# Memory values as column strips on widened probabilities, and token values moved between two projections

## The chip, the cores and the metric

The kernel runs on one core of a Trainium2 chip. Its engines, by the profile's names, are PE (TensorE matmul) with PEld (TensorE weight load), DVE (VectorE), ACT (ScalarE), POOL (GpSimd) and SP (SyncE, which here only issues DMAs). The metric is device time in microseconds for one execution, as the median of several runs. About 0.3% is what a measurement of this kernel tells from no change.

## The reference, cut to what matters

A recurrent attention layer with memory goes over 2048 tokens in 64 segments of 32. Each segment's input is 8 memory rows followed by its 32 tokens. The 8 memory rows of the output are the next segment's memory, so the segments depend on each other. A feed-forward layer with a squared relu follows over all tokens. B = 1, Dm = D = 640, H = 32 heads, Dh = 128, M = 8, seg = 32, F = 1728, all bfloat16.

```python
idx = jnp.arange(L)                      # L = M + seg_len = 40
mask = (idx[:, None] < M) | (idx[:, None] >= idx[None, :])
mem = mem0
for s in range(n_seg):
    xs = x[:, s * seg_len:(s + 1) * seg_len, :]
    h = jnp.concatenate([mem, xs], axis=1)
    q = jnp.einsum('btd,dhe->bhte', h, Wq)
    k = jnp.einsum('btd,dhe->bhte', h, Wk)
    v = jnp.einsum('btd,dhe->bhte', h, Wv)
    scores = jnp.einsum('bhqe,bhke->bhqk', q, k) * scale
    scores = jnp.where(mask[None, None], scores, -1000000000.0)
    p = _softmax(scores, axis=-1)
    o = jnp.einsum('bhqk,bhke->bhqe', p, v)
    o = jnp.einsum('bhte,hed->btd', o, Wo)
    mem = o[:, :M, :]
    outs.append(o[:, M:, :])
...
# then: h = x + attention(layernorm(x)); out = h + relu(layernorm(h) @ w1 + b1)**2 @ w2 + b2
```

## The kernel before

**Stages.** `start()` projects the first segment and the first tails. Then comes a loop of 64 calls of `step(b, sp)`, one for each segment (s = 4b + sp), and last the feed-forward layer in four blocks of 512 tokens (line 918 on). Every engine runs its instructions in the order in which the program writes them (`manual_schedule`, line 109), so the order of the lines is the order in each engine's queue. The number of copies of a tile (`bufs`) and the data decide what waits.

**Rows of a step.** A segment's 40 rows are split into 32 (8 memory rows and the first 24 tokens, the "main" rows) and 8 (the last tokens, the "tail"). The main rows are projected in the step itself. The tails of four segments are projected together, one block ahead, by small units that stand in a list `fill` and are put between other matmuls by `run(fill, n)`. Lists `late`, `mid` and `owed` hold pieces for the other engines, to be run at later places.

**Two forms of matmul.** The 128 x 128 array is used in strips. A projection, a score or a product with Wo loads 128 x 32 weights (written `128*32` in the profile) and four of them work side by side on four column strips. The values (probabilities times v) use `32*128`: 32 rows of v, four side by side on four row strips, one for each group g of 8 heads. Heads are in G = 4 groups of HG = 8, and the partitions 32g to 32g + 31 of a softmax tile hold group g. Two halves n = 0, 1 hold 16 heads each.

**Order of a step on TensorE.** Projections q0, k0, q1, k1 (`project`, line 471: 20 matmuls of 512 columns each, copied out by ACT, turned by DVE into qT and kT). Memory scores of half 0 (`scores(0)`, line 492), v half 0 up to c = 2, token scores of half 0, the rest of v half 0, v half 1 up to c = 2, memory and token scores of half 1, v half 1 c = 2. Then `values(0)`, the rest of v half 1, one fill unit, six rounds of Wo over heads of half 0 (`wo_rounds(main, pw, 0, 6)`, line 619), the token values of the segment before (`token_values(s - 1)`, line 426), `values(1)`, the remaining Wo rounds with fill units between, and more fill units, while DVE and ACT turn the 8 new memory rows into the next step's input (`mem_to_hT`, line 291). The next q0 needs these.

**Memory probabilities.** Only the 8 memory rows' results are needed at once. `soft1(n)` (line 501) takes the maximum on DVE and the exponential on ACT into em (128 x 40: 32 main keys, 8 tail keys), with its sum read out to zm. `soft2(n)` (line 510) on DVE: reciprocal, scale of the main part, a product that spreads the 8 tail keys over 4 x 8 places under the mask `same`, and a 32 x 32 block transpose to pT (128 x 64). `values(n, pT, po)` (line 522) multiplies: for each of 4 heads j and 4 groups g, 32 rows of v times 8 columns of pT; then 4 matmuls for the tail keys with `vt4`, the tail rows' values fetched back from DRAM. `values_out` (line 536) copies po to oT, for n = 0 on DVE, for n = 1 on ACT. Token probabilities take the whole next stretch: tk, mxk on DVE (lines 611 to 615), ek on ACT, zk and rk on DVE, pkt and pk on POOL (lines 632 to 645), turned by DVE in the next step (`owed`, lines 654 to 660). They are used one step later.

**PSUM.** `mm` has three banks in turn, `chn` one for memory scores and the Wo sums `pw`, `po` (four banks) the values.

**Padding.** `align` (line 122) counts the TensorE instructions issued and lets `proj` split some 512-column matmuls into two of 256, so that the number of instructions before a fixed place in each step is a multiple of 256 plus a set number (`PLACE`).

Of the kernel before, what the change touches and what calls it, by code (L numbers as in the profile page):

```python
# [16 lines left out]
def kernel(  # L17
# [16 lines left out]
    nc = tc.nc  # L34
# [44 lines left out]
    o_ring = [const.tile([64, DH], BF16, name="o%d" % k) for k in range(5)]  # L79
# [20 lines left out]
    nc.vector.tensor_copy(out=same[:], in_=diag[:].unsqueeze(2).to_broadcast([128, 4, TL]))  # L100
    qT = const.tile([128, H, NK], BF16)
# [10 lines left out]
    BLOCK, AHEAD, PLACE = 256, 65, 34  # L112
# [189 lines left out]
    fill, late, mid, owed = [], [], [], [[], [], []]  # L302
# [123 lines left out]
    def token_values(s, v, vt4, po, opens):  # L426
# [3 lines left out]
        for i in range(HG):  # L430
            for g in range(G):
                r = slice(32 * g, 32 * g + 32)
                matmul(po[:, g, i * 32:(i + 1) * 32], lhsT=v[r, i * E:(i + 1) * E], rhs=pTk[r, i, :],
                                 start=(opens and i == 0), stop=False, skip_group_check=True)
# [24 lines left out]
    def step(b, sp, v=None):  # L459
# [5 lines left out]
        if not ready:  # L465
            v = vs.pop(0) if vs else s2.tile([128, EG], BF16, tag="v", name="v")
        run(late, 10 if b in (0, NB - 2, NB - 1) else 2)
# [33 lines left out]
        def soft1(n):  # L501
            mx = s2.tile([128, 1], F32, tag="mx", name="mx")
            nc.vector.tensor_reduce(out=mx[:], in_=sms[n][:, 0:NK], op=ALU.max, axis=AX.X, negate=True)  # L503
            em = s2.tile([128, NK], BF16, tag="em", name="em")
            zm = s2.tile([128, 1], F32, tag="zm", name="zm")
            nc.scalar.activation(out=em[:], in_=sms[n][:, 0:NK], func=ACT.Exp, bias=mx[:, 0:1], scale=1.0,  # L506
                                 accum_out=zm[:])
            ems[n], zms[n] = em, zm

        def soft2(n):  # L510
            rm = s2.tile([128, 1], F32, tag="rm", name="rm")
            nc.vector.reciprocal(out=rm[:], in_=zms[n][:])
            pm = s2.tile([128, 2 * SEG], BF16, tag="pmem", name="pmem")
            nc.vector.tensor_scalar(out=pm[:, 0:SEG], in0=ems[n][:, 0:SEG], scalar1=rm[:, 0:1], scalar2=None, op0=ALU.mult)
            nc.vector.scalar_tensor_tensor(out=pm[:, SEG:2 * SEG].rearrange("p (j k) -> p j k", k=TL),
                                           in0=ems[n][:, SEG:NK].unsqueeze(1).to_broadcast([128, 4, TL]),
                                           scalar=rm[:, 0:1], in1=same[:], op0=ALU.mult, op1=ALU.mult)
            pT = s2.tile([128, 2 * SEG], BF16, tag="pTm", name="pTm")
            nc.vector.transpose(out=pT[:], in_=pm[:])
            return pT  # L520

        def values(n, pT, po):
            c0 = 256 + n * 4 * M
            for j in range(4):
                i = n * 4 + j
                for g in range(G):
                    r = slice(32 * g, 32 * g + 32)
                    matmul(po[:, g, c0 + j * M:c0 + (j + 1) * M], lhsT=v[r, i * E:(i + 1) * E],
                                     rhs=pT[r, j * M:(j + 1) * M], start=(i == 0), stop=False,
                                     skip_group_check=True)  # L530
            for g in range(G):
                r = slice(32 * g, 32 * g + 32)
                matmul(po[:, g, c0:c0 + 4 * M], lhsT=vt4[r, sp, n, :], rhs=pT[r, 32:64],
                                 start=False, stop=True, skip_group_check=True)

        def values_out(n, po):
            c0 = 256 + n * 4 * M
            evac(n == 0, oTg[:, n, :, :, 0:M], po[:, :, c0:c0 + 4 * M].rearrange("p g (j m) -> p g j m", m=M))

        if not ready and not last:  # L540
            align(s + b, 4 * 8 * DC + 32 + 1 + 16)
# [3 lines left out]
        run(owed[0], 2)  # L545
        if not last:
            project("k", wk, kT, 0)
        run(owed[1], 2)
        run(late, 1)
        project("q", wq, qT, 1)  # L550
        if last:
# [5 lines left out]
        run(owed[2], 1)  # L557
# [40 lines left out]
        po = pop.tile([128, G, 512], F32, tag="po", name="po")  # L598
        if not ready:
            proj(wv, "half", lhs, 1, ps1, 2, 3)  # L600
        if not last:
            values(0, pT0, po)
            values_out(0, po)
# [11 lines left out]
        nc.vector.tensor_tensor(out=tk[:], in0=tk[:], in1=mxk[:].unsqueeze(2).to_broadcast([128, HG, NK]), op=ALU.subtract)  # L615

        pw = chn.tile([128, 512], F32, tag="ch", name="pw")
        main = lambda p: oT[:, p, 0:32]
        wo_rounds(main, pw, 0, 6)
        if s:  # L620
            token_values(s - 1, prev["v"], prev["vt4"], po, last)
        if not last:
            values(1, pT1, po)
            values_out(1, po)
        wo_rounds(main, pw, 6, 8)
# [7 lines left out]
        nc.scalar.activation(out=ek[:], in_=tk[:], func=ACT.Exp, scale=1.0)  # L633
        zk = s1.tile([128, HG], F32, tag="zk", name="zk")
        nc.vector.tensor_reduce(out=zk[:], in_=ek[:], op=ALU.add, axis=AX.X)  # L635
        if not last:
            mem_to_hT(pw, hT4s[(s + 1) // 4], (s + 1) % 4)
# [8 lines left out]
        if s:  # L646
            owed[0].append(lambda: token_out(0, po))
            owed[1].append(lambda: token_out(1, po))
# [13 lines left out]
        if not last:  # L662
            tails_in((s + 1) // 4, (s + 1) % 4)
# [178 lines left out]
    for b in range(NB):  # L842
        for sp in range(4):
# [34 lines left out]
            if b > 0 and sp == 1 and b + 1 < NB:  # L878
                late.append(lambda b=b: ln_norm(b + 1))
# [29 lines left out]
    token_values(NS - 1, prev["v"], prev["vt4"], po, True)  # L909
# [105 lines left out]
```

## Time and profile before

| what | value |
| --- | --- |
| median of 3 runs | 958.0 us (956.51 to 959.76) |
| the profiled execution, its own time | 958.06 us |
| its span on the core | 956.3 us |
| PE matmul time in the span | 929.1 us, 97% |
| DVE, ACT, POOL busy | 699.7, 548.4, 258.2 us |
| granted TensorE clock | 1.000 |
| a step of the loop (479.70 to 515.80 holds three) | 12.28, 11.95, 11.87 us |
| longest waits of the PE | 12.3 us at the start (xn), 4.8 us for hT over five steps, 1.4, 1.4 and 1.1 us once each |

The profile has one line for each group of instructions. The program's own matmul helper records every matmul, so all matmuls have the line L116, and they are told apart by the tiles they write and read: `ps<-wq,hT` is a projection, `sm<-kT,qz` memory scores, `ps<-kT,qT` token scores, `po<-pTm,v` memory values, `po<-pTk,v` token values (`pTx,vt` and `pTm,vt` their tail keys), `pw<-wo,oT` the product with Wo. A matmul's end is modelled, so the time that TensorE loses between two matmuls is read from where the next one starts, not from its idle time. In the timeline, neighbouring instructions of one group are merged into a line with its count; the columns are start, length, engine, line, operation, tiles and shapes, and in brackets idle time before it and what ended it.

### The profile page before, as it was taken

The numbers are of one execution on the slowest core, as the hardware profiler recorded it, in microseconds if no ns is written. First come the engines' busy times: TensorE is split into PE (matmuls) and PEld (weight loads), VectorE is DVE, ScalarE is ACT, GpSimd is POOL, SyncE is SP. The second block draws the span as 40 slices with busy tenths as digits, with TensorE's granted clock in tenths as the row PEclk, the third lists the DMA queues.
The fourth block names the chain that finished last, engine by engine and source line by source line (L and its number), as shares of the span: only waits on it lengthen the run. The fifth ranks groups of instructions, "written<-read, shape, count | busy, mean of one in ns | idle before, by whom it ended". The sixth has DMA issues, their size and how long they took to land.

```text
span 956.3 us, 57547 instructions
## 1 busy us (share of the span) xinstructions
PE 929.1 (97%) x25874; PEld 570.3 (60%) x25883; DVE 699.7 (73%) x2136; ACT 548.4 (57%) x1343; POOL 258.2 (27%) x798
## 2 busy tenths in 40 slices
PE   4989999999999999999999999999999998999998
PEld 2545666666666666666666666656666665555555
DVE  3167778888888888888887787878787888566532
ACT  2556666666666666666666666656666665523321
POOL 1013222222222222222222222222222233263300
PEclk9999999999999999999999999999999999999999
DMA  9973210101010101010101010101010111643320
GB/s 360 396 235 90 45 29 13 29 13 30 10 33 9 34 10 34 9 34 9 33 10 34 9 32 11 32 11 32 11 32 11 53 43 21 199 113 86 94 56 28
DMA packets 60838, 56.74 MB, mean 59 GB/s; under 512 B 27696, under 2 KB 56752, under 8 KB 58672
## 3 DMA queue, kind: packets, MB, share of 16 engines
q1 hardware_dynamic: 59712, 52.73, 18.3%
q8 instruction: 202, 3.31, 1.5%
q10 hardware_dynamic: 880, 0.34, 0.1%
q14 instruction: 44, 0.36, 0.1%
HBM read 38.37 MB, written 9.44 MB: 50 GB/s over the span
## 4 chain that ended last, share of the span: by engine, by line
PE 93%; DMA 3%; DVE 2%; ACT 1%; issue 1%; ACTq 0%; DVEq 0%
PE ps L116 63%; PE pw L116 16%; PE y L116 6%; PE po L116 5%; DMA vt_d<-row 2%; PE sm L116 1%; PE pa L116 1%; DMA om<-in_A_mem_dram 1%; ACT otc L298 0%; ACTq L157 0%; ACT row L266 0%; DVE otr L297 0%; DVE kTt L269 0%; DVE qT L269 0%; DVE kT L269 0%
## 5 line engine op out<-in xcount | busy, mean ns | idle before, releaser
L116 PEld LDWEIGHTS <-hT 128*32 128x32 bf16 x8383 | 216.9, 96 | 146.2 <-DVE hT L300 20.7
L116 PE MATMUL pw<-wo,oT 128*32 128x320 bf16 x4224 | 178.4, 300 | 0.2
L116 PE MATMUL ps<-wv,hT 128*32 128x512 bf16 x2520 | 177.5, 380 | 0.0
L116 PE MATMUL ps<-wq,hT 128*32 128x512 bf16 (+1 forms) x3168 | 160.6, 336 | 4.8 <-DVE hT L300 4.8
L116 PE MATMUL ps<-wk,hT 128*32 128x512 bf16 (+1 forms) x2575 | 159.7, 375 | 0.0
L641 POOL TENSOR_TENSOR pkt<-ek,rk 128x64 bf16<-128x64 bf16 x64 | 19.3, 301 | 421.7 <-DVE rk L639 408.4
L116 PEld LDWEIGHTS <-oT 128*32 128x32 bf16 x4224 | 100.9, 96 | 44.8 <-ACT oT L257 9.1
L269 DVE STREAM_TRANSPOSE qT<-row 128x512 bf16<-128x512 bf16 x128 | 89.5, 699 | 24.4 <-ACT row L264 20.5
L264 ACT ACTIVATE row<-ps 128x512 bf16<-128x512 f32 (+1 forms) x170 | 93.7, 562 | 13.7 <-PE ps L116 11.7
L937 ACT ACTIVATE wv<-ps,b1f 128x512 bf16<-128x512 f32 (+1 forms) x56 | 37.6, 673 | 66.5 <-PE ps L116 66.0
L442 ACT CAST oT<-po 128x512 bf16<-128x512 f32 x128 | 74.7, 586 | 0.0
L298 ACT COPY otc<-otr 64x40 f32<-64x40 f32 x126 | 28.2, 224 | 71.5 <-DVE otr L297 71.1
L453 POOL COPY qz<-qT 128x96 bf16<-128x96 bf16 x126 | 33.5, 266 | 112.5 <-DVE mx L503 58.2
L116 PEld LDWEIGHTS <-hTt 128*32 128x32 bf16 x1640 | 45.1, 97 | 31.4 <-issue 2.0
L266 ACT CAST row<-ps 128x512 bf16<-128x512 f32 (+1 forms) x113 | 61.6, 560 | 1.9 <-PE ps L116 0.5
L635 DVE TENSOR_REDUCE zk<-ek 128x8 f32<-128x320 bf16 x64 | 31.1, 486 | 42.9 <-ACT ek L633 42.9
L116 PEld LDWEIGHTS <-v 32*128 32x128 bf16 x4064 | 42.1, 91 | 32.8 <-issue 18.4
L116 PE MATMUL y<-wq,wk 128*128 128x320 bf16 x448 | 61.2, 299 | 0.2 <-DVE wk L938 0.2
L484 ACT CAST row<-ps 128x256 bf16<-128x256 f32 x126 | 40.8, 376 | 30.3 <-PE ps L116 30.2
L257 ACT CAST oT<-po 128x128 bf16<-128x128 f32 x63 | 16.8, 267 | 65.3 <-PE po L116 65.3
L606 ACT CAST v<-ps 128x512 bf16<-128x512 f32 x63 | 37.0, 587 | 29.7 <-PE ps L116 29.7
L116 PEld LDWEIGHTS <-qz 128*32 128x32 bf16 x2016 | 36.0, 95 | 28.1 <-ACT em L506 1.9
(109 smaller groups left out, 1659.9 us busy)
## 6 DMA issues: line engine op xcount, KB each, us to landing
wv<-in_A_Wv_dram SPq DMA_DIRECT2D x5, 1024.0 KB
wq<-in_A_Wq_dram SPq DMA_DIRECT2D x5, 1024.0 KB
wk<-in_A_Wk_dram SPq DMA_DIRECT2D x5, 1024.0 KB
vt<-vt_d SPq DMA_DIRECT2D x60, 64.0 KB
xt<-in_A_x_dram SPq DMA_DIRECT2D x18, 160.0 KB
wo<-in_A_Wo_dram SPq DMA_DIRECT2D x2, 1280.0 KB
wo<-in_A_Wo_dram SPq DMA_DIRECT2D x4, 640.0 KB
wq<-in_B_w_dram SPq DMA_DIRECT2D x1, 2080.0 KB
```

Of the source, the lines that this page charges most:

```text
L116: nc.tensor.matmul(*a, **k)
L264: nc.scalar.mul(out=row, in_=ps, mul=scale)
L266: nc.scalar.copy(out=row, in_=ps)
L269: nc.vector.transpose(out=dst[:, n * 16:(n + 1) * 16, 0:32], in_=row.rearrange("p (h e) -> p h e", e=32))
L298: nc.scalar.copy(out=tc_[:, a], in_=tr[64:128, a, :, 0:M])
L442: nc.scalar.copy(out=oTg[:, n, :, :, M:NK], in_=po[:, :, n * 128:(n + 1) * 128].rearrange("p g (j q) -> p g j q", q=32))
L453: nc.gpsimd.tensor_copy(out=d.rearrange("p a (j f) -> p a j f", j=3)[:, :, :, 0:M], in_=src[:, :, 0:3, :])
L484: nc.scalar.copy(out=row[:, u * 256:(u + 1) * 256], in_=ps[:, u * 256:(u + 1) * 256])
L606: nc.scalar.copy(out=v[:, 512:1024], in_=ps1[:])
L635: nc.vector.tensor_reduce(out=zk[:], in_=ek[:], op=ALU.add, axis=AX.X)
L641: nc.gpsimd.tensor_tensor(out=pkt[:], in0=ek[:, :, SEG:NK], in1=rk[:].unsqueeze(2).to_broadcast([128, HG, TL]), op=ALU.mult)
L937: nc.scalar.activation(out=r[:, 0:w], in_=ps[:, 0:w], func=ACT.Relu, bias=b1f[:, fc:fc + 1], scale=1.0)
```

## The change

1. **Memory values of both halves.** The probabilities are multiplied, after the transpose, by a block-diagonal 0/1 mask over the four groups (`gmask`), which makes pw_ of 128 x 2 x 4 x 32: the main part on DVE, the tail part on POOL. The matmuls then contract over all 128 partitions: for each head j and each strip q of 32 values, `v[:, c:c+32]` as weights and 4 x 8 columns; and 4 matmuls of 128 columns for the tail keys. The result of half 0 goes to free columns of the token scores' bank `sk`, that of half 1 to `po`.
2. **Masked tail keys earlier.** The spreading product under `same` moves from DVE, after the reciprocal, to POOL, right after the exponential and before the scaling, which then covers both parts in one instruction.
3. **Token values of the segment before** run between the projections k0 and q1 of the next step, in place of between the Wo rounds. What they need (`owed`: the turning of pkt and pk, pTx, tokens_kept) runs at the head of the step. `token_out` is no longer owed to the next step: half 0 is copied out by ACT after the eighth Wo round, half 1 after mem_to_hT.
4. **Order of smaller pieces.** `tails_in` runs right after token_out(0), no longer at the end of the step. zk comes after mem_to_hT. For blocks after the first, `ln_norm` runs after the token softmax's subtraction (list `between`), not from `late`. Four o buffers in place of five. The padding number and the count given to `align` differ.

```diff
-    o_ring = [const.tile([64, DH], BF16, name="o%d" % k) for k in range(5)]
+    o_ring = [const.tile([64, DH], BF16, name="o%d" % k) for k in range(4)]
...
+    gmask = const.tile([128, G], BF16)
+    nc.vector.tensor_reduce(out=diag[:], in_=ident[:].rearrange("p (g k) -> p g k", k=32), op=ALU.add, axis=AX.X)
+    nc.vector.tensor_copy(out=gmask[:], in_=diag[:])
...
-    BLOCK, AHEAD, PLACE = 256, 65, 34
+    BLOCK, AHEAD, PLACE = 256, 65, 146
...
+        for q in owed:
+            run(q, 2)
         run(late, 10 if b in (0, NB - 2, NB - 1) else 2)
...
-            em = s2.tile([128, NK], BF16, tag="em", name="em")
+            em = s2.tile([128, 2, NK], BF16, tag="em", name="em")
...
-            nc.scalar.activation(out=em[:], in_=sms[n][:, 0:NK], func=ACT.Exp, bias=mx[:, 0:1], scale=1.0,
+            nc.scalar.activation(out=em[:, 0], in_=sms[n][:, 0:NK], func=ACT.Exp, bias=mx[:, 0:1], scale=1.0,
                                  accum_out=zm[:])
+            nc.gpsimd.tensor_tensor(out=em[:, 1, 0:SEG].rearrange("p (j k) -> p j k", k=TL),
+                                    in0=em[:, 0, SEG:NK].unsqueeze(1).to_broadcast([128, 4, TL]), in1=same[:], op=ALU.mult)
...
-            pm = s2.tile([128, 2 * SEG], BF16, tag="pmem", name="pmem")
-            nc.vector.tensor_scalar(out=pm[:, 0:SEG], in0=ems[n][:, 0:SEG], scalar1=rm[:, 0:1], scalar2=None, op0=ALU.mult)
-            nc.vector.scalar_tensor_tensor(out=pm[:, SEG:2 * SEG].rearrange("p (j k) -> p j k", k=TL),
-                                           in0=ems[n][:, SEG:NK].unsqueeze(1).to_broadcast([128, 4, TL]),
-                                           scalar=rm[:, 0:1], in1=same[:], op0=ALU.mult, op1=ALU.mult)
-            pT = s2.tile([128, 2 * SEG], BF16, tag="pTm", name="pTm")
-            nc.vector.transpose(out=pT[:], in_=pm[:])
-            return pT
+            pm = s2.tile([128, 2, SEG], BF16, tag="pmem", name="pmem")
+            nc.vector.tensor_scalar(out=pm[:], in0=ems[n][:, :, 0:SEG], scalar1=rm[:, 0:1], scalar2=None, op0=ALU.mult)
+            pT = s2.tile([128, 2, SEG], BF16, tag="pTm", name="pTm")
+            nc.vector.transpose(out=pT[:].rearrange("p t k -> p (t k)"), in_=pm[:].rearrange("p t k -> p (t k)"))
+            pw_ = s1.tile([128, 2, G, SEG], BF16, tag="pTw", name="pTw")
+            for t, eng in enumerate((nc.vector, nc.gpsimd)):
+                eng.tensor_tensor(out=pw_[:, t], in0=pT[:, t].unsqueeze(1).to_broadcast([128, G, SEG]),
+                                  in1=gmask[:].unsqueeze(2).to_broadcast([128, G, SEG]), op=ALU.mult)
+            return pw_
...
+        def values(n, pT, ps, opens):
+
+            split = lambda x: x.rearrange("p (g j m) -> p g j m", g=G, m=M)
+            main, kept = (pT[:, t].rearrange("p g k -> p (g k)") for t in range(2))
             for j in range(4):
...
+                for q in range(4):
+                    c = (n * 4 + j) * E + 32 * q
+                    matmul(split(ps[32 * q:32 * q + 32])[:, :, j], lhsT=v[:, c:c + 32], rhs=split(main)[:, :, j],
+                           start=(opens and j == 0), stop=False, skip_group_check=True)
+            for q in range(4):
+                matmul(ps[32 * q:32 * q + 32], lhsT=vt4[:, sp, n, 32 * q:32 * q + 32], rhs=kept,
+                       start=False, stop=True, skip_group_check=True)
+            evac(n == 0, oTg[:, n, :, :, 0:M], split(ps))
...
-            align(s + b, 4 * 8 * DC + 32 + 1 + 16)
+            align(s + 3 * b, 4 * 8 * DC + 2 * (G * HG + 2 * G) + 32 + 1 + 16)
         project("q", wq, qT, 0)
         if not last and not ready:
             spread(0)
-        run(owed[0], 2)
         if not last:
             project("k", wk, kT, 0)
-        run(owed[1], 2)
+        po = pop.tile([128, G, 512], F32, tag="po", name="po")
+        if s and not last:
+            token_values(s - 1, prev["v"], prev["vt4"], po)
         run(late, 1)
         project("q", wq, qT, 1)
...
         run(late, 10)
-        run(owed[2], 1)
...
-            values(0, pT0, po)
-            values_out(0, po)
+            values(0, pT0, sk[:, HG * NK:HG * NK + 128], False)
...
+        run(between, 1)
...
         wo_rounds(main, pw, 0, 6)
+        if not last:
+            values(1, pT1, po[:, 0, 256:384], s == 0)
+        wo_rounds(main, pw, 6, 8)
         if s:
-            token_values(s - 1, prev["v"], prev["vt4"], po, last)
+            token_out(0, po)
         if not last:
-            values(1, pT1, po)
-            values_out(1, po)
-        wo_rounds(main, pw, 6, 8)
+            tails_in((s + 1) // 4, (s + 1) % 4)
...
         nc.scalar.activation(out=ek[:], in_=tk[:], func=ACT.Exp, scale=1.0)
+        if not last:
+            mem_to_hT(pw, hT4s[(s + 1) // 4], (s + 1) % 4)
+        if s:
+            token_out(1, po)
...
         nc.vector.tensor_reduce(out=zk[:], in_=ek[:], op=ALU.add, axis=AX.X)
-        if not last:
-            mem_to_hT(pw, hT4s[(s + 1) // 4], (s + 1) % 4)
...
-            owed[0].append(lambda: token_out(0, po))
-            owed[1].append(lambda: token_out(1, po))
             owed[2].append(lambda: tokens_kept(s - 1))
...
-        if not last:
-            tails_in((s + 1) // 4, (s + 1) % 4)
...
-                late.append(lambda b=b: ln_norm(b + 1))
+                between.append(lambda b=b: ln_norm(b + 1))
```

More of the change, by code (lines that the diff above doesn't have):

```diff
@@ L300, in mem_to_hT @@
             nc.vector.tensor_tensor(out=hT4[64 * a:64 * a + 64, :, sp, 0:M], in0=tr[0:64, a, :, 0:M], in1=tc_[:, a], op=ALU.add)
-    fill, late, mid, owed = [], [], [], [[], [], []]
+    fill, late, mid, between, owed = [], [], [], [], [[], [], []]
     def run(q, n):
@@ L424, with token_values @@
     back = []
-    def token_values(s, v, vt4, po, opens):
+    def token_values(s, v, vt4, po):
         sp = s % 4
@@ L433, in token_values @@
                 matmul(po[:, g, i * 32:(i + 1) * 32], lhsT=v[r, i * E:(i + 1) * E], rhs=pTk[r, i, :],
-                                 start=(opens and i == 0), stop=False, skip_group_check=True)
+                                 start=(i == 0), stop=False, skip_group_check=True)
         for u in range(2):
@@ L518, in soft2 @@
-            pT = s2.tile([128, 2 * SEG], BF16, tag="pTm", name="pTm")
-            nc.vector.transpose(out=pT[:], in_=pm[:])
-            return pT
-        def values(n, pT, po):
-            c0 = 256 + n * 4 * M
-            for j in range(4):
[L525 to L534, printed above, removed]
@@ L536, in values_out @@
-        def values_out(n, po):
-            c0 = 256 + n * 4 * M
-            evac(n == 0, oTg[:, n, :, :, 0:M], po[:, :, c0:c0 + 4 * M].rearrange("p g (j m) -> p g j m", m=M))
+            pm = s2.tile([128, 2, SEG], BF16, tag="pmem", name="pmem")
+            nc.vector.tensor_scalar(out=pm[:], in0=ems[n][:, :, 0:SEG], scalar1=rm[:, 0:1], scalar2=None, op0=ALU.mult)
+            pT = s2.tile([128, 2, SEG], BF16, tag="pTm", name="pTm")
+            nc.vector.transpose(out=pT[:].rearrange("p t k -> p (t k)"), in_=pm[:].rearrange("p t k -> p (t k)"))
@@ L544, in step @@
             spread(0)
-        run(owed[0], 2)
         if not last:
             project("k", wk, kT, 0)
-        run(owed[1], 2)
+        po = pop.tile([128, G, 512], F32, tag="po", name="po")
+        if s and not last:
+            token_values(s - 1, prev["v"], prev["vt4"], po)
         run(late, 1)
         project("q", wq, qT, 1)
+        if last:
+            token_values(s - 1, prev["v"], prev["vt4"], po)
         if last:
@@ L597, in step @@
             run(fill, DC)
-        po = pop.tile([128, G, 512], F32, tag="po", name="po")
         if not ready:
@@ L908 @@
     po = pop.tile([128, G, 512], F32, tag="po", name="po")
-    token_values(NS - 1, prev["v"], prev["vt4"], po, True)
+    token_values(NS - 1, prev["v"], prev["vt4"], po)
     for n in range(2):
```

## The prediction

> **What bounds the kernel now.** I read the page first (busy time, chain), then the timeline of one step from 479.4 to 488.7 us, then the matmuls by form and the groups of the other engines.
>
> ```profile
> span 956.3 us, 57547 instructions
> ...
> PE 929.1 (97%) x25874; PEld 570.3 (60%) x25883; DVE 699.7 (73%) x2136; ACT 548.4 (57%) x1343; POOL 258.2 (27%) x798
> ...
> PE 93%; DMA 3%; DVE 2%; ACT 1%; issue 1%; ACTq 0%; DVEq 0%
> ```
>
> TensorE sets the time: busy 97%, 93% of the chain. But its ends are modelled, so small waits hide in "busy". They show in the starts. The timeline of the step (start, length, engine, instruction), cut to what is used below:
>
> ```profile
> 480.54 0.30 ACT L506 ACTIVATE em<-sm,mx 128x40 bf16<-128x40 f32 x1
> ...
> 480.73 0.19 ACT L506 ACTIVATION_READ_ACCUMULATOR em<-sm,mx 128x1 f32 x1
> ...
> 481.15 0.23 DVE L514 TENSOR_SCALAR pmem<-em,rm 128x32 bf16<-128x32 bf16 x1
> 481.30 0.24 DVE L515 SCALAR_TENSOR_TENSOR pmem<-em,rm,same 128x32 bf16<-128x32 bf16 x1
> ...
> 481.54 0.41 PE L116 MATMUL ps<-wv,hT 128*32 128x512 bf16 x4
> 481.58 0.24 DVE L519 STREAM_TRANSPOSE pTm<-pmem 128x64 bf16<-128x64 bf16 x1
> ...
> 481.88 0.26 PE L116 MATMUL po<-pTm,v 32*128 32x8 bf16 x16
> ...
> 482.11 0.61 PE L116 MATMUL ps<-wv,hT 128*32 128x512 bf16 x8
> 482.25 0.29 DVE L255 CAST oT<-po 128x128 bf16<-128x128 f32 x1 [0.34 <-PE po L116]
> ...
> 482.68 0.99 PE L116 MATMUL pw<-wo,oT 128*32 128x320 bf16 x24
> ...
> 483.60 0.37 PE L116 MATMUL po<-pTk,v 32*128 32x32 bf16 x32
> ...
> 484.02 0.20 PE L116 MATMUL po<-pTm,vt 32*128 32x32 bf16 x4
> ...
> 484.15 0.46 PE L116 MATMUL pw<-wo,oT 128*32 128x320 bf16 x8
> ...
> 484.71 1.26 PE L116 MATMUL pw<-wo,oT 128*32 128x320 bf16 x32
> ...
> 487.56 1.25 PE L116 MATMUL ps<-wq,hT 128*32 128x512 bf16 x20
> ...
> 488.64 1.25 PE L116 MATMUL ps<-wk,hT 128*32 128x512 bf16 x20
> ```
>
> Pace: 20 matmuls of 512 columns take 488.64 - 487.56 = 1.08, so a round of four side by side takes 0.215; the 32 of 320 columns run from 484.71 to 485.80 where the next matmul starts, 0.136 a round. Against this pace, two places lose time.
>
> First half of the memory values: the four matmuls at 481.54 have streamed by 481.755; the values start at 481.88 and the projection goes on at 482.105. Together 0.35. Token values and second half: 24 matmuls from 482.68 are through at 483.50; the token values start at 483.60, and the last row-strip round (484.02, worth 0.025) is followed only at 484.15. Together 0.65. In both places about 0.10 is lost each time the tile form changes between 128*32 and 32*128: four changes, 0.4 us a step. At 481.88 one other thing is on time to the hundredth: the transpose of the probabilities ends at 481.82, and TensorE starts 0.06 later. There is no slack there.
>
> **The change, part by part (per step, 62 steps have all of it).**
>
> *Memory values as column strips.* Again 16 + 4 matmuls per half, now 128*32. The 16 take 32 columns; scores of 40 columns in this form go at 16 in 0.10 (481.30 to 481.40), so 0.10. The 4 take 128 columns: 0.215 x 128/512 = 0.06. With no wait a half costs 0.16, without a change of form.
>
> *Token values between k and q.* 40 matmuls in the old form: 0.10 change, 0.22 and 0.07 as at 483.60 to 483.89, 0.10 back: 0.49, against nothing there before. TensorE work alone then goes from 0.35 + 0.65 = 1.00 to 0.16 + 0.16 + 0.49 = 0.81: -0.19 a step, -12 us.
>
> *The longer way to the probabilities, first half.* Old: sum read out 480.92, reciprocal from 480.97, scale 481.15, masked product 481.30, transpose 481.58 to 481.82. New: GpSimd makes the masked copy of em. Its start: 0.06 after the read-out (501.54 + 0.67 to the copy at 502.27 shows such a handover from VectorE), its length 0.24 (pTx, the same shape, 241 ns), so 481.22; with 0.04 back, the scale starts at 481.26 instead of 481.15, takes 0.23, then 0.04 and the transpose 0.24: 481.77. The scalar_tensor_tensor is gone, but a product of 128x128 follows on VectorE. The trace has none of that shape; 128x320 f32 takes 0.49, 64x40 f32 0.19, bf16 128x256 0.33: between 0.22 and 0.35, I take 0.28 from the line through the first two. So 481.81 to 482.09, and TensorE at 482.15: 0.395 after it is free (481.755), since the form change that used to cover 0.10 is gone too. The 16 end at 482.25. GpSimd's product serves the last 4:
>
> ```profile
> L644 POOL TENSOR_TENSOR pk<-ek,rk 128x256 bf16<-128x256 bf16 x64 | 39.8, 622 | 0.0
> ...
> L641 POOL TENSOR_TENSOR pkt<-ek,rk 128x64 bf16<-128x64 bf16 x64 | 19.3, 301 | 421.7 <-DVE rk L639 408.4 <-DVE hn L744 6.7 <-ACT otmp L287 6.6
> ```
>
> Between 301 ns for 64 and 622 for 256 elements, 128 take 0.41: 481.83 to 482.24. But both products read two SBUF operands at once, and the FFN stage shows what that does:
>
> ```profile
> 845.25 0.41 DVE L938 TENSOR_TENSOR wk<-wv 128x512 bf16<-128x512 bf16 x1
> ...
> 845.32 1.59 POOL L749 TENSOR_TENSOR wv<-wk,wq 128x640 f32<-128x640 bf16 x1
> ...
> 869.97 1.39 POOL L749 TENSOR_TENSOR wv<-wk,wq 128x640 f32<-128x640 bf16 x1
> ...
> 870.02 1.63 DVE L938 TENSOR_TENSOR wk<-wv 128x512 bf16<-128x512 bf16 x1
> ```
>
> Whoever starts second pays: VectorE's product grows from 0.41 to 1.63, to past GpSimd's end; GpSimd's grows from 1.39 to 1.59 when VectorE is 0.07 ahead for 0.34 more. In the change VectorE is first by 0.02, so GpSimd loses about 0.26 - 0.14 = 0.12 (0.14 being the part of 0.34 that cost nothing): 482.36, last four at 482.40, projection on at 482.46 instead of 482.105: +0.36. Without this it is 482.35, +0.25.
>
> [...]
>
> *Second half.* Let W be when the projection goes on. TensorE is at these values at W + 1.40 (two rounds of 512, one of 320, six of 320, as before: 482.105 to 483.50). VectorE first waits to copy the first half out (last matmul to copy 0.25 before; 0.27 with the longer matmul; 0.29 long), and behind it in its queue stand reciprocal 0.15, scale, transpose, product, each with 0.04 between: W + 1.60, with 0.06 more main at W + 1.66, through at W + 1.76; GpSimd's product after the transpose at W + 1.29: 0.06 + 0.41 + 0.12 + 0.03, last four at W + 1.91, TensorE on at W + 1.97. So 0.57 here, 0.26 of it wait for VectorE and 0.15 for GpSimd. Token values used to stand in front and covered this way; they have moved.
>
> *Sum per step:* (482.46 - 481.755) 0.705 + 0.57 + 0.49 = 1.765 against 1.00: +0.76, x 62 = 47 us. Without the sharing of operands 0.595 + 0.45 + 0.49: +0.53, 33 us. The cost to a GpSimd that is second rests on one kind of row; I take 42 us, most of the way to the first.
>
> *What lies beside other work.* token_out(0) stands ahead of ek on ScalarE and token_out(1) ahead of otmp, 0.58 each. ek ends near 486.1, the memory copies (L298) are due at 486.7 then; otmp comes 0.5 later, and only o and its store wait. In four-step turns ln_norm (0.41) stands between tk and otr on VectorE: tk is through near 485.6, otr due near 486.4, so 0.35 is left; without that cover each such step pays 0.41. zk after mem_to_hT puts rk, pkt, pk and pTk later: from hT, 0.03 + 0.49 + 0.03 + 0.20 + 0.15 + 0.30 + 0.60 + 0.05 + 0.41 + 0.06 = 2.32; TensorE needs pTk after two projections and a change, 0.05 + 2.16 + 0.10 = 2.31. Just in time where nothing stands ahead of q, so 0; 0 to 0.2 in the range. tails_in and tokens_kept move to idle stretches of GpSimd (27% busy); no DMA is issued elsewhere on SP's queue. Four o buffers instead of five: each is written again after four outputs, over 36 us, and its store is issued at once: 0. The padding number changes which matmuls are halved: 17 more pairs in all, and halves stream as fast; TensorE's recorded waits for issue are 1.3 us in the run: 0 to 3 us.
>
> The profiled execution took 958.06 (span 956.3), the median of the runs is 958.0, so the sum stands on either: 958 + 42 = 1000.
>
> Bounds. Low: the masked copy starts at the exponential's own end (480.84), product 0.22, no sharing: +0.26 a step, 16 us, 974. High: handovers to GpSimd of 0.15 (rk to pkt), product 0.35, GpSimd wholly behind it: +1.16 a step, 72 us, 1030.
>
> **Rivals.**
> *The longer way is covered, only the form changes count* (faster): -0.19 x 62, 946. For it: the four changes are real in each step. Against it: the probabilities would have to be there at 481.78, earlier than today, on a longer way. It decides once the waits of both halves stay under 0.19 together.
> *Half the waits* (both engines start early, operands not shared): the low bound, 974.
> *Token values wait too:* pk is GpSimd's last of a row that starts later; 0.2 more in each step on top of the forecast is 12 us, 1012. For it the margin of 0.01; against it the steps with a tail output, where q starts 0.4 after hT.
> *Gains and waits cancel*: 958.
>
> **How the numbers follow.** Forecast 0.60, half the waits 0.15, token values late 0.12, covered 0.10, cancel 0.03. About 0.3% is what a measurement of this kernel tells from no change. Slower 0.87, faster 0.10, same 0.03. The range 968 to 1022 holds the first three but for the upper end of the bounds.
>
> **What would show it.** TensorE's starts: values of the first half some 0.4 after the four matmuls ahead are through, behind pTw L526 of VectorE; the last four behind GpSimd's; the same near W + 1.66; around the second half no 0.10 of a form change is left. GpSimd's pTw longer than 0.41 shows the sharing. Wrong if main values start within 0.1 of TensorE being free, or if GpSimd's masked copy ends before the reciprocal.

## The result, and the profile after

The changed kernel takes 1009.4 us (median of 4 runs, 1008.2 to 1010.2) against 958.3 us (4 runs, 956.5 to 959.8): a ratio of 1.0534, with a 95% interval of 1.0513 to 1.0554. It is slower by 51 us. The profiled execution of the changed kernel took 1009.49 us, its span is 1007.7.

The page of the changed kernel: the span; busy time, share and instructions of the engines; the chain of work that ended last, by engine.

```profile
span 1007.7 us, 57930 instructions
...
PE 962.7 (96%) x25891; PEld 573.9 (57%) x25900; DVE 720.1 (71%) x2138; ACT 547.9 (54%) x1343; POOL 339.8 (34%) x1050
...
PE 67%; DVE 12%; ACT 10%; issue 4%; POOL 3%; DMA 2%; ACTq 0%; DVEq 0%; SPq 0%; POOLq 0%
```

TensorE's busy share has hardly moved (97% to 96%). Its share of the chain has: 93% before, 67% now, with DVE, ACT and POOL in its place. So TensorE now waits for the others, though "busy" doesn't show it. The list of waits of the same kernel (who waits for whom: us in total, times, longest) has one new long entry:

```profile
PE ps L119 <- DVE pTw L526: 12.2, 60, 0.5
```

The timeline of one step of the changed kernel shows both halves (start, length, engine, line, instruction; idle time before it and what ended it):

```profile
508.79 0.19 ACT L511 ACTIVATION_READ_ACCUMULATOR em<-sm,mx 128x1 f32 x1
...
509.06 0.24 POOL L513 TENSOR_TENSOR em<-em,same 128x32 bf16<-128x32 bf16 x1 [0.44 <-ACT em L511]
...
509.33 0.24 DVE L521 TENSOR_SCALAR pmem<-em,rm 128x64 bf16<-128x64 bf16 x1 [0.16 <-POOL em L513]
...
509.60 0.41 PE L119 MATMUL ps<-wv,hT 128*32 128x512 bf16 x4
509.61 0.24 DVE L523 STREAM_TRANSPOSE pTm<-pmem 128x64 bf16<-128x64 bf16 x1
...
509.89 0.29 DVE L526 TENSOR_TENSOR pTw<-pTm,gmask 128x128 bf16<-128x128 bf16 x1
510.03 0.41 POOL L526 TENSOR_TENSOR pTw<-pTm,gmask 128x128 bf16<-128x128 bf16 x1 [0.73 <-DVE pTm L523]
...
510.24 0.28 PE L119 MATMUL ps<-pTw,v 128*32 128x32 bf16 x16 [0.23 <-DVE pTw L526]
...
510.49 0.24 PE L119 MATMUL ps<-pTw,vt 128*32 128x128 bf16 x4
...
510.55 0.62 PE L119 MATMUL ps<-wv,hT 128*32 128x512 bf16 x8
...
511.13 1.00 PE L119 MATMUL pw<-wo,oT 128*32 128x320 bf16 x24
...
511.80 0.29 DVE L526 TENSOR_TENSOR pTw<-pTm,gmask 128x128 bf16<-128x128 bf16 x1
...
511.94 0.41 POOL L526 TENSOR_TENSOR pTw<-pTm,gmask 128x128 bf16<-128x128 bf16 x1 [0.85 <-DVE pTm L523]
...
512.15 0.28 PE L119 MATMUL po<-pTw,v 128*32 128x32 bf16 x16
...
512.40 0.24 PE L119 MATMUL po<-pTw,vt 128*32 128x128 bf16 x4
512.46 0.46 PE L119 MATMUL pw<-wo,oT 128*32 128x320 bf16 x8
```

Read it backwards from TensorE. The four matmuls of 509.60 have streamed at 509.81. The main values can start only at 510.24, 0.06 after DVE's product ends (509.89 + 0.29 = 510.18). The last four start at 510.49, 0.05 after POOL's product ends (510.03 + 0.41 = 510.44). At 512.15 and 512.40 the same two waits come again (511.80 + 0.29 = 512.09, and 511.94 + 0.41 = 512.35); there no token values stand in front any more. No tenth is lost to a change of form on either side of the values.

The step, from its first q matmul to the next step's, by the position of the segment in its block of four (medians): 11.90, 11.96, 11.92, 12.38 us before; 12.67, 12.89, 12.68, 13.27 after. That is about 0.83 a step. From the first of these steps to the last, 62 in all, the changed kernel takes 50.5 us longer: nearly the whole difference is in the loop.

One loss was not foreseen. The projections of a step of the changed kernel, same view:

```profile
502.23 0.57 ACT L445 CAST oT<-po 128x512 bf16<-128x512 f32 x1
...
502.60 1.27 PE L119 MATMUL ps<-wq,hT 128*32 128x512 bf16 x35
502.82 0.42 ACT L290 COPY otmp<-pw 64x320 f32<-64x320 f32 x1
...
503.27 0.86 ACT L269 CAST row<-ps 128x512 bf16<-128x512 f32 x2
...
503.91 0.61 PE L119 MATMUL ps<-wk,hT 128*32 128x512 bf16 x8
```

ACT copies token_out(1) (502.23) and otmp (502.82) before the result of the fill unit (503.27 to 503.86, the first of the two merged copies). This copy frees the PSUM bank that k0 needs. Where nothing waits, a q0 that is split like this one takes 1.10 and would be through at 503.71. The fill unit's copy ends at 503.86, and k0 starts at 503.91. In two of the four positions, where a fill unit ends just there, k0 comes 0.19 late.

### The profile page after: what moved, and what is told of

Its sections match the earlier page's. It is cut to its first block, busy times and chain, and to the rows that moved or that the text cites. A ratio compares the mean times of both kernels' runs of the same rounds, so it can differ in the third digit from the quotient of the medians.

```text
span 1007.7 us, 57930 instructions
## 1 busy us (share of the span) xinstructions
PE 962.7 (96%) x25891; PEld 573.9 (57%) x25900; DVE 720.1 (71%) x2138; ACT 547.9 (54%) x1343; POOL 339.8 (34%) x1050
## 4 chain that ended last, share of the span: by engine, by line
PE 67%; DVE 12%; ACT 10%; issue 4%; POOL 3%; DMA 2%; ACTq 0%; DVEq 0%; SPq 0%; POOLq 0%
PE ps L119 40%; PE pw L119 14%; PE y L119 6%; PE po L119 5%; ACT row L267 4%; DVE qT L272 3%; ACT em L511 2%; ACT otc L301 2%; DVE pTw L526 2%; DVE otr L300 2%; DVE pTm L523 2%; DVE pmem L521 2%; POOL em L513 1%; DMA vt_d<-row 1%; POOL qz L456 1%
## 5 line engine op out<-in xcount | busy, mean ns | idle before, releaser
L119 PEld LDWEIGHTS <-hT 128*32 128x32 bf16 x8400 | 204.9, 96 | 148.3 <-DVE hT L303 23.5
L119 PEld LDWEIGHTS <-oT 128*32 128x32 bf16 x4224 | 104.1, 96 | 45.2 <-ACT oT L260 14.4
L119 PEld LDWEIGHTS <-v 128*32 128x32 bf16 (+1 forms) x4064 | 50.6, 92 | 66.2 <-issue 51.3
L526 POOL TENSOR_TENSOR pTw<-pTm,gmask 128x128 bf16<-128x128 bf16 x126 | 52.7, 418 | 100.6 <-DVE pTm L523 97.6
L300 DVE STREAM_TRANSPOSE otr<-pw 128x160 f32<-128x160 f32 x126 | 36.6, 328 | 53.5 <-PE pw L119 41.5
L511 ACT ACTIVATE em<-sm,mx 128x40 bf16<-128x40 f32 x126 | 37.0, 293 | 42.4 <-DVE mx L508 39.9
```

Of the source, the lines that this page charges most:

```text
L119: nc.tensor.matmul(*a, **k)
L300: nc.vector.transpose(out=tr[:, a], in_=blocks[:, a])
L511: nc.scalar.activation(out=em[:, 0], in_=sms[n][:, 0:NK], func=ACT.Exp, bias=mx[:, 0:1], scale=1.0, accum_out=zm[:])
L526: eng.tensor_tensor(out=pw_[:, t], in0=pT[:, t].unsqueeze(1).to_broadcast([128, G, SEG]), in1=gmask[:].unsqueeze(2).to_broadcast([128, G, ...
```

## The experiments

The theory after the result: the 51 us are two waits at the memory values, for the two products that widen the probabilities; the form changes are a small term. Rivals: the sharing of operands between DVE and POOL; the moved token values; the small pieces that were reordered.

**1. No wait for the products.** The strip matmuls read a constant; the products are still formed.

```diff
-            main, kept = (pT[:, t].rearrange("p g k -> p (g k)") for t in range(2))
+            main, kept = ident[:], ident[:]
```

> The changed kernel, but the strip matmuls of both halves read a constant tile in place of the widened probabilities; the products are still formed, nobody waits for them (so the memory values are not the reference's). Theory (the time went into TensorE's waits for the widened probabilities): the waits of 0.385 + 0.157 at the first half and about 0.13 + 0.157 at the second, as the trace of the changed kernel shows them, go: 0.83 a step, about 50 us, so 955 to 965. Rival (the strips and the two forms of matmul cost the time themselves, or the token values do): the time stays above 1000.

Measured: 977.5 us, ratio to before 1.0206 (1.0191 to 1.0221). The time lies between the two expectations: the waits at the values are gone and bring 32 us, but 19 more than before are still there. The waits and the timeline of this kernel show where:

```profile
PE ps L119 <- DVE hT L303: 15.7, 47, 1.4
```

```profile
507.72 0.47 ACT L639 ACTIVATE ek<-tk 128x320 bf16<-128x320 f32 x1 [0.51 <-DVE tk L619]
508.22 0.58 DVE L300 STREAM_TRANSPOSE otr<-pw 128x160 f32<-128x160 f32 x2 [0.54 <-ACT ek L639]
...
509.34 0.40 PE L119 MATMUL ps<-wq,hT 128*32 128x512 bf16 x4 [0.24 <-DVE hT L303]
```

The products still stand in DVE's queue ahead of tk. So tk and ek come late against a TensorE that no longer waits, and the turn of the new memory rows (otr, which shares tk's buffer) waits 0.54 for ek to have read it. The next step's q0 waits for that turn. A wait taken away had hidden a second cost of the same products.

There is a second such place. In three of the four positions the first Wo rounds start 0.16 to 0.27 late, 0.05 after ScalarE's read-out of the second half's em ends. Their sums `pw` need the PSUM bank of the memory scores (`chn` has one), which the exponential that makes em must have read; and it waits for the maximum (mx), which stands behind the product in DVE's queue.

The constant also spares TensorE the wait for the transpose, which stands ahead of the products. In the step of the changed kernel shown above the transpose ends at 509.85, and with 0.06 for the way TensorE could start at 509.91, 0.10 after it is free; in the other positions it is 0.06. By this estimate some 4 of the 32 us belong to the transpose and not to the products.

**2. The token values moved and the small pieces reordered**; the memory values stay row strips, with soft2 and values as before.

```diff
-        def values(n, pT, ps, opens):
+        def values(n, pT, po):
...
-            split = lambda x: x.rearrange("p (g j m) -> p g j m", g=G, m=M)
```

> The changed kernel with the memory values of the kernel before (row strips, old softmax path, results in po): the move of the token values and the smaller pieces alone. Theory: six changes of form in place of four (+0.2 a step, 12 us) and two waits that the smaller pieces bring (0.07 in three of four steps before the next q, 0.2 in two of four steps before k, together 0.15 a step, 9 us): 975 to 985. Rival (the move is harmless and all of the loss is in the widened probabilities): 958 to 962.

Measured: 974.4 us, 1.0173 (1.0158 to 1.0188), 17 us slower than before and just under the range expected. The first half takes 0.57 a step as before, the token values in their new place 0.385 with 0.12 ahead of them for the change of form, and k0's wait of 0.19 is there in the same two positions. This move brings two more changes of form and k0's wait.

**3. Only the strips.** The kernel before with column strips and widening, token values in their old place.

```diff
+        if s and not last:
+            token_values(s - 1, prev["v"], prev["vt4"], po)
...
-        po = pop.tile([128, G, 512], F32, tag="po", name="po")
-        if s and not last:
-            token_values(s - 1, prev["v"], prev["vt4"], po)
         run(late, 1)
```

> The kernel before with the column strips, masked copy on GpSimd and widened probabilities, token values where they were between the rounds of Wo. Theory: the first half pays as in the changed kernel, +0.34 a step; at the second half the token values cover most of the wait, and the changes of form are two there as before: 0 to +0.05. So 20 to 25 us, 978 to 984, less than half of the whole loss. Rival (the strips alone are the loss, 0.5 a step or more whatever stands in front): 995 to 1010.

Measured: 983.8 us, 1.0272 (1.0255 to 1.0289), 26 us slower. The first half costs +0.37 a step (0.33 to 0.42 by position), about as in the changed kernel (+0.35). The second half doesn't wait: its main values take 0.115 there against 0.257 in the changed kernel, since the token values in front cover the way. Alone the two parts cost 17 and 26 us, together 51: the rest of 8 is the wait of the second half, which only shows when both are made.

**4. The small pieces back**: zk ahead of mem_to_hT, token_out(1) behind the fill unit and the output.

```diff
-        if not last:
-            mem_to_hT(pw, hT4s[(s + 1) // 4], (s + 1) % 4)
-        if s:
-            token_out(1, po)
         nc.vector.tensor_reduce(out=zk[:], in_=ek[:], op=ALU.add, axis=AX.X)
+        if not last:
+            mem_to_hT(pw, hT4s[(s + 1) // 4], (s + 1) % 4)
```

> The changed kernel with zk ahead of mem_to_hT again and the second copy of the token values behind the copies that free the Wo sums and the fill units' banks. Theory (both orders cost on their own: the turn of the memory rows starts 0.07 later after the last round of Wo because it then waits for two engines, and k0 waits 0.2 for a bank whose copy stands behind token_out(1) in two of four steps): 0.15 a step back, 9 us, 998 to 1002. Rival (these are only shifts of waits that come back elsewhere): 1007 to 1011.

Measured: 1006.5 us, 1.0507 (1.0491 to 1.0523). k0's wait of 0.19 is gone in both positions, so ACT's order was its cause. But zk now stands ahead of the turn and waits for the late ek: the turn starts 0.50 after the last Wo matmul instead of 0.42. The net is 3 us instead of the 7 to 11 expected. Moving zk was right in this kernel; moving token_out(1) was not.

**5. Is POOL slowed by DVE?** DVE's product is left out, POOL's stays.

```diff
-            for t, eng in enumerate((nc.vector, nc.gpsimd)):
+            for t, eng in ((1, nc.gpsimd),):
...
-            main, kept = (pT[:, t].rearrange("p g k -> p (g k)") for t in range(2))
+            main, kept = ident[:], pT[:, 1].rearrange("p g k -> p (g k)")
```

> The changed kernel without VectorE's product of the widened probabilities: the main strip matmuls read a constant tile in its place, GpSimd's product for the tail keys stays (so the memory values are not the reference's). In the changed kernel GpSimd's product starts 0.17 after the transpose's end and takes 0.415. If it is held up by VectorE's product, which reads two SBUF operands at the same time, it starts 0.06 to 0.09 after the transpose now, and TensorE's last four matmuls of a half come 0.08 to 0.11 earlier. If 0.17 is the plain way from VectorE to GpSimd, it stays at 0.17.

Measured: one execution, 1005.8 us. The timeline of this kernel, transpose and POOL's product:

```profile
507.13 0.25 DVE L523 STREAM_TRANSPOSE pTm<-pmem 128x64 bf16<-128x64 bf16 x1
...
507.54 0.40 POOL L526 TENSOR_TENSOR pTw<-pTm,gmask 128x128 bf16<-128x128 bf16 x1 [0.72 <-DVE mx L508]
```

POOL's product starts 0.169 after the transpose's end (mean over the steps; 0.170 in the changed kernel), so the product on DVE doesn't delay its start. But its length shows the slowing. Without DVE's product it takes 0.40 wherever it starts. With DVE's product it ends 0.584 after the transpose's end, whether it starts 0.17, 0.14 or 0.08 after it, and so takes 0.413, 0.439 or 0.505 (medians over the ten traces that have both products). Experiment 1 has rows with the early start:

```profile
503.88 0.25 DVE L523 STREAM_TRANSPOSE pTm<-pmem 128x64 bf16<-128x64 bf16 x1
...
504.16 0.29 DVE L526 TENSOR_TENSOR pTw<-pTm,gmask 128x128 bf16<-128x128 bf16 x1
504.20 0.50 POOL L526 TENSOR_TENSOR pTw<-pTm,gmask 128x128 bf16<-128x128 bf16 x1 [0.64 <-DVE pTm L523]
```

DVE's product ends 0.327 after the transpose, and POOL's ends 0.257 behind that each time. So POOL's product is held until DVE's is through, all but the first 0.14 of its 0.40. In the changed kernel, where it mostly starts at 0.17, that costs only 0.014. The main values no longer wait here, but the last four do, and so the time stays within 4 us: the wait for POOL's product alone sets it.

**6. Token values ahead of values(0)**, so that they cover the first half's way.

```diff
-        if s and not last:
-            token_values(s - 1, prev["v"], prev["vt4"], po)
...
+        if s and not last:
+            token_values(s - 1, prev["v"], prev["vt4"], po)
         if not last:
             values(0, pT0, sk[:, HG * NK:HG * NK + 128], False)
```

> The changed kernel with the token values right ahead of the memory values of the first half, not between k0 and q1. Theory (the first half's loss is a wait of fixed length that any TensorE work can cover): 0.29 of token values and 0.2 of form changes now stand where TensorE waited 0.385 + 0.157, so 0.45 to 0.5 a step come back, 27 to 30 us: 978 to 984. Rival (the wait moves with the work in front of it, because the chain to the probabilities is itself held by TensorE): 1000 or more.

Measured: 988.1 us, 1.0306 (1.0287 to 1.0324), 21 us less than the changed kernel and a little above what was expected. The main wait of the first half is gone; the last four still come late in some positions (the block of main values lasts 0.12 to 0.24, against 0.257); the second half waits as before. So in the first half the wait is the rest of a way of fixed length, and TensorE work in front of it shortens it.

**7. Strips for the second half alone**, where the Wo rounds cover the way; the token values in row strips right ahead of values(0), so that only two changes of form are left.

```diff
+        if s and not last:
+            token_values(s - 1, prev["v"], prev["vt4"], po, True)
         if not last:
-            values(0, pT0, po)
+            values(0, pT0, po, not s)
...
-            values(1, pT1, po)
-            values_out(1, po)
+            strips(1, pT1, po[:, 0, 320:448])
```

> The kernel before, with the token values ahead of the memory values of the first half (still row strips), the second half alone as column strips with the widened probabilities (masked product on VectorE as before), and the first half copied out by ScalarE, so that VectorE's way to the second half need not wait for it. Theory (a form change costs 0.1 and the widened probabilities cost only where TensorE waits for them): two form changes in place of four, -0.2 a step, and the second half's probabilities are there at 483.7 of the step shown where TensorE wants them at 483.8, so no wait: 944 to 950. Rival (the second half waits here too, or the longer way on VectorE holds tk and so the next q): 958 or more.

Measured: 975.6 us, 1.0174 (1.0152 to 1.0197), a miss by 25 us. The second half does what it should (0.10 and 0.055, no wait, no tenth for a form), but TensorE stands still elsewhere. The timeline of this kernel:

```profile
495.06 0.31 PE L119 MATMUL ps<-wo,oTt 128*32 128x320 bf16 x4
...
495.84 1.00 PE L119 MATMUL pw<-wo,oT 128*32 128x320 bf16 x24 [0.48 <-issue]
```

The four matmuls of 495.06 are one round, worth 0.136, and the 24 should start at 495.20. Nothing that they read is late; "issue" means that the profile shows no releaser. About once a step such a stop of 0.4 to 0.7 appears. Its place is fixed. Count two instructions for each matmul (its weight load and itself) and one for each that TensorE's sequencer executes itself (95 in the run): all 53 gaps of over 0.34 us between two starts in the loop that do not wait for hT then stand at place 192 or 193 in a row of 256. (Seven of them are put down to ScalarE's copy of v, which those matmuls do not read.) Less 0.21 each, the usual pace, they add up to 24 us, nearly the whole miss. The expectations below put the place at 112 to 160; counted without the sequencer's instructions it slides from 186 to 112 through the run. The kernel's own padding keeps such a place fixed in the step. It was set for another count of instructions.

**8. The products not formed at all** (experiment 1 with soft2 returning before them).

```diff
-            for t, eng in enumerate((nc.vector, nc.gpsimd)):
-                eng.tensor_tensor(out=pw_[:, t], in0=pT[:, t].unsqueeze(1).to_broadcast([128, G, SEG]),
...
-            return pw_
+            return None
```

> As the run with the constant tile (977.5), but neither product is formed any more. There the waits for the probabilities went and 18 us of the expected 50 stayed: the next step's input waits longer after the last round of Wo (0.42 in place of 0.23), since tk, ek and the turn of the memory rows stand behind the products on VectorE. Theory (VectorE's queue is the next limit): tk comes 0.3 earlier, the turn 0.2, and the first half's copy no longer stands behind a product: 958 to 970. Rival (what stays is the move of the token values and the strips): 974 to 979.

Measured: 959.8 us, 1.0016 (1.0006 to 1.0026). From the changed kernel to experiment 1 to this one: 1009.4, 977.5, 959.8. The way through the two products costs 50 us: 32 in TensorE's waits (some 4 of them for the transpose, by the estimate in experiment 1) and 18 through DVE's queue, half of it at the turn of the memory rows and half at the first Wo rounds (0.15 a step each). q0's waits for hT are back at 4.6 us over five steps. In the second position of a block, whose step is 0.11 longer than before, TensorE's own work shows the gain that the prediction gave it: 0.41 less around the values, 0.22 more for the token values in their new place (0.10 in the block, 0.12 for the change of form), -0.19. But k0 pays 0.19 and the stretch behind the last Wo rounds 0.11.

**9 to 12. The padding number.** Experiment 7 with other values of PLACE; each step of 16 moves the multiple of 256 by 16 instructions along the step.

```diff
-    BLOCK, AHEAD, PLACE = 256, 65, 34
+    BLOCK, AHEAD, PLACE = 256, 65, 198
```

> As the run with strips in the second half alone (975.6), with the padding number at 198 in place of 34. There TensorE stood still once a step for 0.4 to 0.65 with no wait but issue in the profile, always at an instruction number near 112 to 160 above a multiple of 256, now just behind 120 instructions of token and memory values that run in 0.5 us. Theory (the next 256 instructions are not there yet; 256 of them should take about 3.1 us or more): 164 later puts one such border 92 instructions earlier, into the token values, and splits the fast stretch, so the stop shrinks to 0 to 0.15: 950 to 958. Rival (the stop has another cause, such as ScalarE's copies): 973 to 978.

> The same with 182: the border 16 instructions earlier than with 198. Theory: by the stream of the step the 256 instructions behind it take 2.8 us in place of 3.0, so the stop is 0.1 to 0.3: 955 to 967. Rival: as with 34, 973 to 978.

> The same with 214: the border 16 instructions later than with 198. Theory: the 256 in front of it take 2.7 us, so the stop is 0.2 to 0.4: 960 to 972. Rival: as with 34, 973 to 978.

> The same with 230. From 182 over 198 to 214 the time went 963.9, 959.0, 955.4, so the border is better later than my sum of the stream has it. Theory (what is left are stops of 0.15 to 0.3 in a third of the steps, between the first rounds of Wo, which go as the border moves on): 952 to 955.5. Rival (the 256 instructions in front of the border become the short ones, as my sum has it from 214 on): 957 or more.

| PLACE | time, us | ratio to before |
| --- | --- | --- |
| 34 | 975.6 | 1.0152 to 1.0197 |
| 182 | 963.9 | 1.0043 to 1.0075 |
| 198 | 959.0 | 1.0002 to 1.0025 |
| 214 | 955.4 | 0.9962 to 0.9983 |
| 230 | 970.6 | 1.0124 to 1.0169 |

The same work takes 955 to 976 us by where the multiples of 256 fall. In these five kernels and the kernel before, all 126 gaps of over 0.34 us with no releaser but issue (or that copy of v) stand at place 192 or 193 of a row of 256, whatever work is there: Wo rounds at 182, 198 and 214, mostly memory values at 230, several kinds at 34. So ScalarE's copies are not the cause. That 256 instructions need about 3.1 us was the author's estimate, on which the expectations for 198, 182 and 214 rest. No run shows it: in experiment 7 the rows that end in a stop took 2.6 to 3.8 us. 182 came out as expected, 198 1 us above its range. The turn from falling to rising lies 16 instructions later than the sum for 214 and 230 had it: 214 was expected slower, 230 best. At 214 TensorE's waits for issue are 1.9 us in the whole run, against 13.6 at 34. This is the fastest version found. It is 0.27% faster than before, with an interval that leaves out 1, but less than the 0.3% that a measurement here can tell from no change.

## Why the prediction was right, and where it was off

**What bounds the kernel; the place of the loss: right.** The wait sits where the prediction put it. The wait for DVE's product, the second one for POOL's, the change of form that is no longer paid at the values, and the repeat of both waits in the second half are all in the timeline. Experiments 1 and 8 show that the way through the products carries the loss.

**First half: right to 0.01 in the mean.** Forecast +0.36 a step. Measured from start to start: the last four projection matmuls 0.35 to 0.61, the main values 0.11 to 0.27, the last four 0.11 to 0.055, with 0.01 back in the projection behind, in all +0.35. Masked copy on POOL 0.24 as forecast, DVE's product 0.29 for 0.28, main values 0.43 after TensorE is free in the fourth position, which the step of the forecast has, and 0.38 in the others: 0.395 in the mean, as forecast.

**POOL slowed by DVE's product: right, two terms mis-sized.** The prediction added 0.06 for the way to POOL, from the row of one copy, and 0.12 for the sharing of operands. The way is 0.17 in most rows (experiment 5). POOL then meets less of DVE's product, and the slowing costs only 0.014. The prediction's rule for it, the overlap less 0.14, holds: it gives 0.327 - 0.17 - 0.14 = 0.02 here, and 0.04 and 0.11 for starts at 0.14 and 0.08, where 0.04 and 0.105 were measured. By luck the two sums are nearly one (0.18 and 0.18). The upper bound had POOL wholly behind DVE's product. The traces show POOL held to the end of DVE's product (its own ends 0.257 later and takes 0.40 alone), all but its first 0.14. That it comes from the operands which both read is not shown: experiment 5 takes DVE's product away as a whole.

**Second half: mis-sized.** Forecast 0.57 a step. Measured 0.52 in the fourth position, and 0.45 in the other three (0.14 over pace before the main values, 0.257, 0.055): 0.47 in the mean. Counted from W (where the projection goes on behind the first half), the transpose ends at 1.22 and not 1.29, since the reciprocal starts 0.08 before the end of the first half's copy, where the forecast had it 0.04 behind; so the main values start at W + 1.60 and not 1.66. And the forecast took the fourth position for all: in the other three the round between has 512 columns and not 320 and covers 0.07 more.

**Token values between k0 and q1: right.** Forecast 0.49; measured 0.117 for the change of form and 0.386. The rival that they wait too fell: TensorE waits for pTk in four of 62 steps, 0.04 in two and 0.14 in the last two.

**"otmp comes 0.5 later, and only o and its store wait": wrong.** The fill unit's copy stands behind otmp in ACT's queue, and with it the PSUM bank of k0. That costs 0.19 in two of four positions, 0.09 in the mean; experiment 4 shows it by taking it away.

**The turn of the memory rows: missed.** It starts 0.42 after the last Wo matmul starts, 0.35 before, and with 0.05 for the later copy of the second half the stretch behind it is 0.11 longer in three positions and 0.05 shorter in the fourth: 0.07 in the mean. The 0.42 comes with the order of zk and not with the products: experiments 2 and 8 have it without any product, and experiment 3, with zk in front as before, has 0.35. Why the order costs 0.07 is not shown. The prediction looked at ek against the copies of otc and not at otr, which needs tk's buffer back. Experiment 1 shows how near this lies: with TensorE's waits gone, otr waits 0.54 for ek.

**The sum.** Measured: +0.35 in the first half; the second place with the token values from 0.67 to 0.47 + 0.50, +0.30; k0 +0.09; the turn +0.07; together 0.81 of the 0.83 seen in the steps. The prediction's sum was 0.76, and it then took 42 us where its own 0.76 x 62 is 47. Two errors of opposite sign, the second half (0.10 too dear) and the two queues on ACT and DVE (0.16 left out), nearly cancel. What is left, and taking 42 in place of 47, made the forecast 9 us short. So the range held the result for the right cause, but part of the closeness is luck.

**The rival "covered".** It fell for the changed kernel. Without the products (experiment 8) the rest of the change gives 959.8, not the 946 of that rival: the 0.19 a step is real, but it is paid out again at k0 (0.19 in two positions), behind the last Wo rounds (0.11 in three) and by 0.16 behind the main values of the first position. There the first matmul on the block's tail values (vt4) stands behind waits for three DMAs, which by the trace had landed over 4 us before; why it costs 0.16 is open. No run took all three away, so whether 946 can be had is open.

## What to carry to other kernels

A change of form on TensorE costs a tenth of a microsecond here (0.10 in the kernel before, 0.12 in experiments 2 and 8); a chain of small operations on other engines ahead of it costs more, because a product of 128 x 128 with its handover takes 0.3 to 0.6 here (from the transpose's end to its own: 0.327 on DVE, 0.584 on POOL). Before a shorter way on TensorE is paid for with a step on another engine, ask what TensorE has to do in the meantime: where token values (experiment 3, second half: main values 0.115) or, with the first half copied by ScalarE, Wo rounds (experiment 7: 0.10) stood in front, the same products cost next to nothing; where too little stood there they set the time (0.257 to 0.27 for the same values in the changed kernel). And when an engine's queue gets a new instruction, follow the two next consumers behind it, buffers included (a PSUM bank freed late, 0.19 at k0; a tile tag shared by two uses, 0.54 at otr in experiment 1), not only the one that is named in the change.

## What the hardware showed that was not expected

TensorE stops for 0.4 to 0.7 us at one place of a row of 256 of its own instructions (192 or 193 by the count in experiment 7) when nothing it reads is late. It does not stop in every row; where that place falls in the step moved the same work from 955.4 to 975.6 us. The period agrees with the way the instructions come in. The page of the changed kernel has this among its DMA queues (packets, MB, share of 16 engines' span):

```profile
q8 instruction: 203, 3.33, 1.4%
```

That is 16.4 KB a packet, and the page's 25891 matmuls and 25900 weight loads make 202.3 rows of 256; in the kernel before it is 202 packets for 202.2 rows. By this estimate one packet comes for each row. That a stop is the wait for such a packet is only argued: no run shows one that came late.

POOL's product of 128 x 128, started during DVE's (0.29 us), ends 0.257 after DVE's does, wherever it started between 0.08 and 0.17 after the transpose, and takes 0.41 to 0.51 in place of 0.40 (medians over the ten traces that have both products).

The way from DVE's end to POOL's start is not one number: 0.17 in most rows for these products, 0.14 for the first half of each block's first step in the changed kernel, 0.08 in 30 rows of the ten traces, 0.06 for a copy in the kernel before. What decides it is not shown.
